# A fused adaLN block with its gradients: 128-row chunks for the modulation products, and masks, sums and output pieces moved in the tail

## The chip, the cores and the metric

The kernel runs on one core of one Trainium2 chip, in one launch. The metric is the time of an execution on the device in microseconds; lower is better. The core has a matrix engine (TensorE, PE in the profile, whose weight loads are listed as PEld), a vector engine (DVE), a scalar engine (ACT), GpSimd (POOL) and a queue engine (SyncE, SP) that issues most of the transfers here.

## The reference, cut to what matters

The block works on x of 2048 rows and 576 columns in bfloat16. A conditioning row c gives six modulation rows. The first branch, A, is a spectral filter; the second, B, is a bilinear gated unit with 4608 hidden columns.

```python
mod = (silu(c) @ w_mod).reshape(1, 6, 1, 576)        # c: 1 x 576, w_mod: 576 x 3456
sa, ca, ga, sb, cb, gb = (mod[:, i] for i in range(6))
h = layernorm(x) * (1 + ca) + sa
x = x + ga * irfft2(rfft2(h) * (w_r + 1j * w_i))     # branch A, w_r and w_i: 2048 x 289
h = layernorm(x) * (1 + cb) + sb
x = x + gb * (((h @ w_gate) * (h @ w_up)) @ w_down)  # branch B, w_gate and w_up: 576 x 4608
```

The outputs are this x and, for a given grad_out of the same shape, the gradients of the input x, w_r, w_i, w_gate, w_up, w_down, c and w_mod.

## The kernel before, in words

All on-chip data lie in one hand-planned buffer, which the profile calls `arena`; the eight banks of the matrix engine's output are `bank`. The order of TensorE's instructions is the order of the Python code. The other engines' instructions are put into an order by a scheduler, and each engine then runs its own list strictly in that order. SP issues its transfers from such a list, with eight rotating semaphores, so an issue can also wait for the transfer that was issued eight before it.

**Front (0 to about 160 us).** SP loads grad_out in four parts (`load_go`), x in four (`load_xs`), w_mod in three (`load_wm`: `wm_a` holds the row gb, `wm_b` sa and ca, `wm_c` ga, sb and cb), blocks of w_down (`load_wdn`) and the tables of the transforms (`TB`, `TC`, `TI`, `TBI`). Matmuls with one column turn c into columns (L269, L275, L278); ACT and DVE make silu(c) of them (`sc_bf`). The row gb is needed as a column, and L303 makes it from `wm_a`: five blocks of 128 columns, each a sum over six blocks of 96 rows of w_mod. The other five rows come from `mod_rows` (L328 to L340): for each half row of 288 columns, L333 adds six matmuls over blocks of 96 rows, with silu(c) repeated over 128 columns (`sc_rep`) as weights, so that every partition gets the row. ACT copies one half, DVE the other. `turn_go` transposes grad_out and `evac_go` copies it scaled by gb, `turn_wd` (L262) transposes w_down. The stages of the forward transform (`stage_a`, `stage_b`, `stage_c`, `stage_ci`, `stage_bi`, `stage_ai`) are interleaved with pieces of the product of grad_out and w_down.

**Middle (242 to 1190 us).** A loop over 18 chunks of 256 hidden columns computes branch B and the gradients of its weights.

**Tail (1190 us to the end).** Pieces of independent matmuls fill gaps. They stand in a queue, an object of class `Fill`: `run(us)` adds that many microseconds of credit and takes pieces, each with a nominal cost, until the credit is used up; `left()` is the nominal cost that is left; `flush()` takes all. Two kinds of pieces matter here. Gradient pieces compute the rest of the weight gradients of w_gate and w_up (eight matmuls of 256 or 288 columns, 0.87 us each). y pieces (`y_piece`, L1077) compute the product with w_down that makes the output x: 128 pieces of nine matmuls of 288 columns, 1.1 us each.

1. *Row loop*, 18 steps for 16 blocks of 128 rows. It ends the gradient of h (`gh2_last`), goes back through the second layer norm (`row_front`, `row_back`), adds column sums and products for the modulation gradients (`row_sums`) and starts the backward transform (`row_a`, with `stage_a`). Between them stand two calls `if fill.left() > 9.0: fill.run(1.0)` (L1141, L1145).
2. *Masks and sums.* `diag_mask` and `col_mask` (L1187 to L1203) cut diagonals out of the sums with DVE. Then eight matmuls (L1207) spread them over the partitions, and ACT copies the rows out (L1208).
3. *Spectral loop*, s = 0 to 8 (L1266 to L1298). Each step has `stage_b(s)` (L442), a transposition of the filter `W` (`turn`, L516), then for u = s - 1 `stage_c(u)` (L468, L504), `multiply` (DVE up to L528), the filter's gradient `grad_W` of the step before (DVE, L1249 to L1253) and `stage_ci(u)` (L555). Pieces stand between these by `fill.run`. At s = 1 the rest of the gradient pieces is taken, the queue is changed to the y pieces, and `X_d`, the spectrum that the forward part had stored in DRAM, is loaded for `grad_W` (`load_X`). The results of the gradient pieces are stored to DRAM (L888).
4. *Last loop*, j = 0 to 16 (L1330 to L1366). `stage_bi(j)`, then for row block j - 1 `stage_ai` (L572 and after), its copy out of the bank by ACT (L1341), the normalised x (L1343, made in the ring `x_r` of three buffers, into which SP loads x), the backward layer norm (`ln_bwd_a`, `ln_bwd_b`, with ACT's L1010 among its steps), and `column_sums` (L1031), with y pieces between by `fill.run(2.5)`, twice.
5. *End* (L1369 to L1401). The sums become columns, the gradient of w_mod's gb block is made (`o8l`), the gradient of c is computed from the transposed w_mod (L1391, L1397) and stored. y pieces stand in between by `fill.run(4.0)`.

Of the kernel before, what the change touches and what calls it, by code (L numbers as in the profile page):

```python
# [22 lines left out]
D = 576  # L23
# [58 lines left out]
def build(ctx, tc, A_x, A_w_r, A_w_i, B_w_gate, B_w_up, B_w_down, c_in, w_mod, grad_out,  # L82
# [22 lines left out]
    bank = psp.tile([128, 8, 512], FP32, name="bank")  # L105
# [44 lines left out]
    gbcol, c_f, sig = small[:, 66:71], small[:, 82:88], small[:, 88:94]  # L150
    nt = small[:, 100:108]
    smallb = V(8640, [32])
    c_bf, sc_bf, gb_bf, c2_bf = smallb[:, 0:6], smallb[:, 6:12], smallb[:, 12:17], smallb[:, 17:31]
    go = V(GO, [16, D])
    h2p = V(H2P, [16, 640])
    h2T = V(H2T, [16, 5, 128])
# [38 lines left out]
    TC = V(ACC + 2912, [9, 4, 128])  # L195
    TI = V(ACC + 12128, [9, 4, 128])
    TBI = V(ACC + 21344, [5, 288])
    wm_a, wm_b, wm_c = V(ST, [6, D]), V(ST + 71168, [6, 2 * D]), V(ST + 6912, [6, 3 * D])
    wm_t = {SGB: wm_a, SSA: wm_b[:, :, 0:D], SCA: wm_b[:, :, D:], SGA: wm_c[:, :, 0:D], SSB: wm_c[:, :, D:2 * D], SCB: wm_c[:, :, 2 * D:]}
    sc_rep = V(ST + 27648, [6, 128])  # L200
# [7 lines left out]
    with tc.manual_schedule(engines={PE}):  # L208
# [2 lines left out]
        ac.dma_start(BD.rearrange("p a b -> p (a b)"), tabs["BD"][:, :])  # L211

        def load_wm(t, s0, s1):
            sp.dma_start(t[0:96], w_mod[:, s0 * D:s1 * D].rearrange("(m q) n -> q m n", q=96))

        def load_go(jg):
            sp.dma_start(go[:, 4 * jg:4 * jg + 4, :], go_v[:, 4 * jg:4 * jg + 4, :])
# [1 line left out]
        def load_xs(jg):  # L219
            sp.dma_start(xs[:, 4 * jg:4 * jg + 4, :], x_v[:, 4 * jg:4 * jg + 4, :])  # L220
# [8 lines left out]
        load_go(2)  # L229
        load_go(3)  # L230
        load_xs(0)
        load_wm(wm_b, 0, 2)
        load_wdn(1)
        load_xs(1)
        load_xs(2)
        load_wdn(2)
# [26 lines left out]
                ac.copy(t[:, m0:m1, :].rearrange("p m f -> p (m f)"), pt[:, 0:256 * (m1 - m0)])  # L263


        q96 = slice(0, 96)
        cp = bank[:, 5, 128:160]
        for m in range(6):
            mm(cp[0:96, m:m + 1], c_row[0:1, 96 * m:96 * m + 96], ones[0:1, 0:1], True, True)  # L269
        ve.tensor_copy(c_f[q96], cp[q96, 0:6])  # L270
        act(sig[q96], c_f[q96], ACT.Sigmoid)
        tt(sc_bf[q96], c_f[q96], sig[q96], MUL)
        for h in range(2):
            for m in range(9):
                mm(cp[64 * h:64 * h + 64, 8 + m:9 + m], c_row[0:1, 64 * m:64 * m + 64], ones[0:1, 0:1], True, True)  # L275
        for m in range(5):
            n = 128 if m < 4 else 64
            mm(cp[0:n, 17 + m:18 + m], c_row[0:1, 128 * m:128 * m + n], ones[0:1, 0:1], True, True)  # L278

        def turn_go(jg, m):  # L280

# [17 lines left out]
            turn_go(0, m)  # L299
        for dk in range(5):  # L300
            d0 = 448 if dk == 4 else 128 * dk
            for m in range(6):
                mm(bank[:, 5, dk:dk + 1], wm_a[0:96, m, d0:d0 + 128], sc_bf[0:96, m:m + 1], m == 0, m == 5)  # L303
        ve.tensor_copy(gb_bf[:], bank[:, 5, 0:5])
        ve.tensor_copy(gbcol[:], gb_bf[:])
        c2f = small[:, 82:96]
        ve.memset(c2f, 0.0)
        ve.tensor_copy(c2f[:, 0:13], cp[:, 8:21])
        ve.tensor_copy(c2f[0:64, 13:14], cp[0:64, 21:22])
        for m in range(5):  # L310
            turn_go(1, m)
            evac_go(0, m)
# [1 line left out]
        for jg in (2, 3):  # L314
            for m in range(5):
                turn_go(jg, m)
                if jg == 3:
                    evac_go(1, m)
        for m in range(6):
            ve.tensor_copy(sc_rep[q96, m, :], sc_bf[q96, m:m + 1].to_broadcast([96, 128]))  # L320

        sbank = [0]

# [4 lines left out]
        def mod_rows(s):  # L328
            bias = 1.0 if s in (SCA, SCB) else 0.0
            for h in range(2):  # L330
                b = single()
                for m in range(6):
                    mm(bank[:, b, 0:288], sc_rep[0:96, m, :], wm_t[s][0:96, m, 288 * h:288 * h + 288], m == 0, m == 5)  # L333
                dst = mod[:, s, 288 * h:288 * h + 288]
                if h == 0:
                    act(dst, bank[:, b, 0:288], ACT.Copy, bias=bias)
                elif bias:
                    ts(dst, bank[:, b, 0:288], bias, None, ADD)
                else:
                    ve.tensor_copy(dst, bank[:, b, 0:288])  # L340

        def silu_columns():

            s2 = small[:, 50:64]
            act(s2, c2f, ACT.Sigmoid)
            tt(c2_bf[:, :], c2f, s2, MUL)
# [781 lines left out]
        for j in range(18):  # L1128
            want = min(16, 2 + 5 * j // 4)
            while done < want:  # L1130
                gh2_last(done)
                done += 1
                if done < want:
                    fill.run(1.0)
            while loaded < min(done, j + 3):
                load_n(loaded)
                loaded += 1
            if j < 16:
                row_front(j)
                row_back(j)  # L1140
            if fill.left() > 9.0:  # L1141
                fill.run(1.0)
            if 2 <= j < 18:
                row_sums(j - 2)
            if fill.left() > 9.0:  # L1145
# [12 lines left out]
        load_wdr(28, 36)  # L1158
        sring = [4, 5]


        for k in range(2):
            load_hl(k)
# [37 lines left out]

        m_sga, m_scb, m_ssb, gbh = diag_mask(5, 64), diag_mask(2, 0), col_mask(192), mk_r.next()
        ve.tensor_copy(gbh[:], gbacc[:])  # L1203
        for rows, hi, lo in ((rows23, m_sga, m_ssb), (rows45, m_scb, gbh)):
            for h in range(2):
                for q0, src in ((0, hi), (64, lo)):
                    mm(bank[q0:q0 + 64, 6 + h, 0:288], ones[:, 0:64], src[:, 288 * h:288 * h + 288], True, True)  # L1207
            ac.copy(halves(rows), bank[:, 6:8, 0:288])  # L1208
# [29 lines left out]
        for u in range(2):  # L1238
            Ws[u] = W_r.next()
            load_W(sp, Ws[u], u)  # L1240

        def load_X(u):
            Xls[u] = Xl_r.next()
# [86 lines left out]
        for j in range(17):  # L1330
# [6 lines left out]
            if j:  # L1337
                jj = j - 1
                stage_ai(Hs[jj])
                gh = gh_r.next()  # L1340
                ac.copy(halves(gh), bank[:, 2:4, 0:288])  # L1341
                n = xl[jj]
                act(n[:], n[:], ACT.Identity, bias=nmr1[:, jj:jj + 1], scale=rstd1[:, jj:jj + 1])  # L1343
# [116 lines left out]
```

## Time and profile before

| | us |
|---|---|
| median of four runs (1536.87, 1532.36, 1526.55, 1533.34) | 1532.85 |
| the profiled execution's own time | 1527.39 |
| its span, first to last instruction | 1525.5 |
| TensorE busy | 1476.6 |
| VectorE busy | 782.9 |
| ScalarE busy | 557.2 |
| GpSimd busy | 262.4 |

The profiled execution is one execution, and lies 5.5 us under the median of the runs. Times inside the profile count from the start of its span. A line such as "PE bank L555 <- DVE arena L528: 5.5, 4, 4.3" says that TensorE's instructions of line 555, which write a bank, waited four times for line 528 on VectorE, 5.5 us in total and 4.3 at the longest. A line of the stretches gives its bounds and length, then for each engine the busy time with the number of its instructions (PE, PEld, DVE, ACT, POOL), the clock granted to TensorE (1.00 is full), the DMA engines' share and the GB/s that they moved. A line of an engine's timeline gives the start, the duration, the instruction, and in brackets the idle time before it with what ended that.

### The profile page before, as it was taken

To read this page: it belongs to the slowest core of one execution; us is meant where nothing else is said; L and a number is where in the kernel's file an instruction comes from. 1 tells how busy PE (TensorE), PEld (TensorE's weight loads), DVE (VectorE), ACT (ScalarE), POOL (GpSimd) and SP (SyncE) were. 2 spreads that over 40 slices of the span, in tenths; PEclk is the share of its full clock that TensorE was granted. 3 is DMA by queue.
4 is the path that set the end of the run, shared out by engine and by line. 5 is a ranking of instruction groups with operands and counts; after the bars stand their busy time and mean duration, and the time that the engine had idled before them with its cause. 6 is when DMAs were issued, how large, how long until landed. Compare 5 with 4: busy or idle time off the path is not lost.

```text
span 1525.5 us, 28468 instructions
## 1 busy us (share of the span) xinstructions
PE 1476.6 (97%) x11295; PEld 987.5 (65%) x11295; DVE 782.9 (51%) x1733; ACT 557.2 (37%) x1062; POOL 262.4 (17%) x384
## 2 busy tenths in 40 slices
PE   7999998999999999999999999999999998899997
PEld 5444443677667668668668667767767676677665
DVE  6533596543443443453353353354354884787555
ACT  5766675212221221220320321221221674334665
POOL 1222322203202202202211211311301101000000
PEclk9999999999999999999999999999999999999999
DMA  9746886878548547557657646755844689798752
GB/s 295 217 142 160 231 229 165 216 113 189 125 93 185 132 109 162 134 113 156 146 113 145 159 115 130 165 122 119 173 116 92 166 217 290 188 242 206 199 165 86
DMA packets 440967, 248.65 MB, mean 163 GB/s; under 512 B 318401, under 2 KB 418306, under 8 KB 440322
## 3 DMA queue, kind: packets, MB, share of 16 engines
q1 hardware_dynamic: 417570, 176.43, 51.4%
q0 software_dynamic: 22496, 69.62, 15.0%
q8 instruction: 88, 1.44, 0.4%
q10 hardware_dynamic: 768, 0.79, 0.2%
q14 instruction: 45, 0.37, 0.1%
HBM read 96.46 MB, written 74.20 MB: 112 GB/s over the span
## 4 chain that ended last, share of the span: by engine, by line
PE 75%; issue 17%; DVE 3%; ACT 2%; DMA 2%; SPq 0%; POOL 0%; POOLq 0%; DVEq 0%; ACTq 0%
PE bank L802 9%; PE bank L833 8%; PE bank L804 8%; PE bank L880 8%; PE bank L884 8%; PE bank L939 5%; PE bank L942 5%; PE bank L941 5%; PE bank L940 5%; PE bank L370 3%; PE bank L374 3%; PE bank L797 3%; PE bank L900 2%; PE bank L858 1%; DMA arena<-in_B_w_down_dram 1%
## 5 line engine op out<-in xcount | busy, mean ns | idle before, releaser
L953 DVE TENSOR_TENSOR arena<-arena,bank 128x576 f32<-128x576 f32 x256 | 193.0, 754 | 305.2 <-PE bank L942 305.2
L808 ACT CAST arena<-bank 128x512 bf16<-128x512 f32 x144 | 84.3, 585 | 386.9 <-PE bank L798 375.3
L939 PE MATMUL bank<-arena 128*128 128x288 bf16 x576 | 164.6, 286 | 0.9 <-ACT arena L885 0.7
L942 PE MATMUL bank<-arena 128*128 128x288 bf16 x576 | 165.2, 287 | 0.0
L941 PE MATMUL bank<-arena 128*128 128x288 bf16 x576 | 165.0, 286 | 0.0
L940 PE MATMUL bank<-arena 128*128 128x288 bf16 x576 | 164.7, 286 | 0.0
L880 PE MATMUL bank<-arena 128*128 128x256 bf16 x1152 | 150.4, 274 | 0.5 <-ACT arena L885 0.5
L884 PE MATMUL bank<-arena 128*128 128x256 bf16 x1152 | 150.0, 273 | 0.0
L1077 PE MATMUL bank<-arena 128*128 128x288 bf16 x1152 | 149.7, 287 | 0.0
L802 PE MATMUL bank<-arena 128*128 128x512 bf16 x576 | 148.6, 380 | 0.0
L804 PE MATMUL bank<-arena 128*128 128x512 bf16 x576 | 147.8, 379 | 0.0
L1077 PEld LDWEIGHTS <-arena 128*128 128x128 bf16 x1152 | 111.8, 98 | 31.7 <-issue 3.3
L833 PE MATMUL bank<-arena 128*128 128x288 bf16 x1024 | 128.1, 286 | 0.0
L880 PEld LDWEIGHTS <-arena 128*128 128x128 bf16 x1152 | 111.2, 98 | 17.7 <-issue 4.4
L884 PEld LDWEIGHTS <-arena 128*128 128x128 bf16 x1152 | 112.6, 98 | 14.8 <-issue 1.3
L885 ACT CAST arena<-bank 128x256 bf16<-128x256 f32 x144 | 53.5, 372 | 185.8 <-PE bank L884 185.8
L833 PEld LDWEIGHTS <-arena 128*128 128x128 bf16 x1024 | 100.2, 98 | 28.2
L812 DVE TENSOR_TENSOR arena<-arena 128x512 bf16<-128x512 bf16 x144 | 61.2, 425 | 104.6 <-ACT arena L808 102.3
L802 PEld LDWEIGHTS <-arena 128*128 128x128 bf16 x576 | 50.3, 98 | 78.0 <-issue 30.4
L804 PEld LDWEIGHTS <-arena 128*128 128x128 bf16 x576 | 56.4, 98 | 67.9
L809 ACT CAST arena<-bank 128x512 bf16<-128x512 f32 x144 | 84.8, 589 | 23.1 <-PE bank L804 23.1
L382 ACT CAST arena<-bank 128x1024 bf16<-128x1024 f32 x72 | 72.7, 1013 | 42.0 <-PE bank L378 19.6
(254 smaller groups left out, 2249.0 us busy)
## 6 DMA issues: line engine op xcount, KB each, us to landing
ghh_d<-arena POOLq DMA_DIRECT2D x72, 256.0 KB, 3.8
arena<-ghh_d POOLq DMA_DIRECT2D x36, 512.0 KB, 5.6
hh_d<-arena SPq DMA_DIRECT2D x36, 512.0 KB, 4.5
arena<-hh_d SPq DMA_DIRECT2D x16, 1152.0 KB, 6.9
out_dram<-arena POOLq DMA_DIRECT2D x36, 256.0 KB, 5.1
arena<-in_B_w_down_dram POOLq DMA_DIRECT2D x18, 288.0 KB, 4.1
out_dram<-arena POOLq DMA_DIRECT2D x36, 144.0 KB, 5.5
arena<-in_B_w_gate_dram POOLq DMA_DIRECT2D x18, 256.0 KB, 3.5
```

The costliest lines, as they stand in the source:

```text
L802: mm(bank[:, bg, :], w[:, m, fs], h2T[:, js, m, :], odd == 0 and m == 0, odd == 1 and m == 3)
L804: mm(bank[:, bu, :], w[:, 4 + k, fs], h2T[:, js, m, :], odd == 0 and k == 0, odd == 1 and k == 3)
L809: ac.copy(u[:], bank[:, bu, :])
L833: mm(bank[:, b0 + h, 0:288], sf[:, 0, fb, j, :], go[:, j, 288 * h:288 * h + 288], j == 0, j == 15)
L880: mm(bank[:, st["b"], 0:256], h2p[:, j, 128 * m:128 * m + 128], sf[:, 1 + w, :, j, :], j == 0, False)
L884: mm(bank[:, st["b"], 0:256], h2p[:, j, 128 * m:128 * m + 128], sf[:, 1 + w, :, j, :], False, j == 15)
L939: mm(o, xT[:, 1, 0, cs], wT[p][:, 0, 0, hs], True, False)
L940: mm(o, xT[:, 2, 0, cs], wT[p][:, 0, 1, hs], False, False)
L941: mm(o, xT[:, 1, 1, cs], wT[p][:, 1, 0, hs], False, False)
L942: mm(o, xT[:, 2, 1, cs], wT[p][:, 1, 1, hs], False, True)
L953: tt(dst, dst, src, ADD)
L1077: mm(bank[:, yb, 0:288], hl[:, fb % 18, 128 * (j % 2):128 * (j % 2) + 128], wdr[:, fb, 288 * h:288 * h + 288], fb == 0, fb == 35)
```

## The change

The products with w_mod go over five blocks of rows, four of 128 and one of 64, in place of six of 96 (list `KC`). Each `load_wm` becomes two transfers. L303 has 25 matmuls for 30, L333 60 for 72, the column matmuls 23 for 29. The second block of w_down is loaded ahead of `wm_b`.

In the tail, the thresholds of the row loop go from 9.0 to 11.0, which in the built kernel keeps two gradient pieces longer: twelve for ten are left behind the row loop. The sums of L1207 and L1208 become a function `spread`, called twice in step s = 0 of the spectral loop with a gradient piece between; two gradient pieces stand ahead of `stage_b(0)`. At s = 1 the gradient pieces are all taken first, and three y pieces follow ahead of `stage_ci(0)`. The loads of w_down's last rows and of the first hidden rows (`load_wdr(28, 36)`, `load_hl`) are written after those of the filter.

In the last loop `fill.run(2.5)` becomes `fill.run(2.2)`, twice. In the built kernel each row block then has four y pieces; before, seven had four and nine had five. Two more y pieces are taken ahead of this loop, and eight for one stand in the end: four ahead of the R2 columns and four between them and L1391.

```diff
@@ load_wm
-            sp.dma_start(t[0:96], w_mod[:, s0 * D:s1 * D].rearrange("(m q) n -> q m n", q=96))
+            sp.dma_start(t[:, 0:4], w_mod[0:512, s0 * D:s1 * D].rearrange("(m q) n -> q m n", q=128))
+            sp.dma_start(t[0:64, 4], w_mod[512:576, s0 * D:s1 * D])
@@ loads
         load_xs(0)
+        load_wdn(1)
         load_wm(wm_b, 0, 2)
-        load_wdn(1)
@@ silu(c) as columns
-        q96 = slice(0, 96)
+        KC = [(0, 128), (128, 128), (256, 128), (384, 128), (512, 64)]
...
-        for m in range(6):
-            mm(cp[0:96, m:m + 1], c_row[0:1, 96 * m:96 * m + 96], ones[0:1, 0:1], True, True)
-        ve.tensor_copy(c_f[q96], cp[q96, 0:6])
-        act(sig[q96], c_f[q96], ACT.Sigmoid)
-        tt(sc_bf[q96], c_f[q96], sig[q96], MUL)
+        for m, (k0, n) in enumerate(KC):
+            mm(cp[0:n, 9 + m:10 + m], c_row[0:1, k0:k0 + n], ones[0:1, 0:1], True, True)
+        ve.tensor_copy(c2f[:, 9:13], cp[:, 9:13])
+        ve.tensor_copy(c2f[0:64, 13:14], cp[0:64, 13:14])
+        act(s2[:, 9:14], c2f[:, 9:14], ACT.Sigmoid)
+        tt(sc_bf, c2f[:, 9:14], s2[:, 9:14], MUL)
@@ gb as a column, mod_rows
-            for m in range(6):
-                mm(bank[:, 5, dk:dk + 1], wm_a[0:96, m, d0:d0 + 128], sc_bf[0:96, m:m + 1], m == 0, m == 5)
+            for m, (_, n) in enumerate(KC):
+                mm(bank[:, 5, dk:dk + 1], wm_a[0:n, m, d0:d0 + 128], sc_bf[0:n, m:m + 1], m == 0, m == 4)
...
-                for m in range(6):
-                    mm(bank[:, b, 0:288], sc_rep[0:96, m, :], wm_t[s][0:96, m, 288 * h:288 * h + 288], m == 0, m == 5)
+                for m, (_, n) in enumerate(KC):
+                    mm(bank[:, b, 0:288], sc_rep[0:n, m, :], wm_t[s][0:n, m, 288 * h:288 * h + 288], m == 0, m == 4)
@@ row loop (both places)
-            if fill.left() > 9.0:
+            if fill.left() > 11.0:
                 fill.run(1.0)
@@ masks and sums
-        for rows, hi, lo in ((rows23, m_sga, m_ssb), (rows45, m_scb, gbh)):
+        def spread(rows, hi, lo):
             for h in range(2):
@@ ahead of the spectral loop
             load_W(sp, Ws[u], u)
+        load_wdr(28, 36)
+        for k in range(2):
+            load_hl(k)
@@ spectral loop
             if s < 8:
+                if s == 0:
+                    fill.run(1.8)
                 Zs[s] = stage_b(s, ac_r, z_r)
                 fill.run(1.0)
                 if s:
                     turn(Ws[s], 6)
+                else:
+                    spread(rows23, m_sga, m_ssb)
                 fill.run(1.2)
+                if s == 0:
+                    spread(rows45, m_scb, gbh)
...
-                fill.run(5.0)
-                if s == 1:
+                if s > 1:
+                    fill.run(5.0)
+                else:
                     fill.flush()
                     fill = yfill
...
+                    fill.run(3.0)
                 stage_ci(u, Y_t, SD_t, Gt)
@@ last loop
-                fill.run(2.5)
-            fill.run(2.5)
+                fill.run(2.2)
+            fill.run(2.2)
```

More of the change, by code (lines that the diff above doesn't have):

```diff
@@ L149, in build @@
     rstd2, nmr2 = small[:, 50:66], small[:, 66:82]
-    gbcol, c_f, sig = small[:, 66:71], small[:, 82:88], small[:, 88:94]
+    gbcol = small[:, 66:71]
     nt = small[:, 100:108]
     smallb = V(8640, [32])
-    c_bf, sc_bf, gb_bf, c2_bf = smallb[:, 0:6], smallb[:, 6:12], smallb[:, 12:17], smallb[:, 17:31]
+    sc_bf, gb_bf, c2_bf = smallb[:, 0:5], smallb[:, 12:17], smallb[:, 17:31]
     go = V(GO, [16, D])
@@ L197, in build @@
     TBI = V(ACC + 21344, [5, 288])
-    wm_a, wm_b, wm_c = V(ST, [6, D]), V(ST + 71168, [6, 2 * D]), V(ST + 6912, [6, 3 * D])
+    wm_a, wm_b, wm_c = V(ST, [5, D]), V(ST + 71168, [5, 2 * D]), V(ST + 6912, [5, 3 * D])
     wm_t = {SGB: wm_a, SSA: wm_b[:, :, 0:D], SCA: wm_b[:, :, D:], SGA: wm_c[:, :, 0:D], SSB: wm_c[:, :, D:2 * D], SCB: wm_c[:, :, 2 * D:]}
-    sc_rep = V(ST + 27648, [6, 128])
+    sc_rep = V(ST + 27648, [5, 128])
     c_row = V(H2T + 6912, [D])
@@ L263, in turn_wd @@
                 ac.copy(t[:, m0:m1, :].rearrange("p m f -> p (m f)"), pt[:, 0:256 * (m1 - m0)])
-        q96 = slice(0, 96)
+        KC = [(0, 128), (128, 128), (256, 128), (384, 128), (512, 64)]
+        c2f, s2 = small[:, 82:96], small[:, 50:64]
+        ve.memset(c2f, 0.0)
         cp = bank[:, 5, 128:160]
-        for m in range(6):
-            mm(cp[0:96, m:m + 1], c_row[0:1, 96 * m:96 * m + 96], ones[0:1, 0:1], True, True)
-        ve.tensor_copy(c_f[q96], cp[q96, 0:6])
-        act(sig[q96], c_f[q96], ACT.Sigmoid)
-        tt(sc_bf[q96], c_f[q96], sig[q96], MUL)
+        for m, (k0, n) in enumerate(KC):
[4 more added lines that the diff above has]
+        tt(sc_bf, c2f[:, 9:14], s2[:, 9:14], MUL)
         for h in range(2):
             for m in range(9):
[L275 to L278, printed above, removed]
+                mm(cp[64 * h:64 * h + 64, m:m + 1], c_row[0:1, 64 * m:64 * m + 64], ones[0:1, 0:1], True, True)
         def turn_go(jg, m):
@@ L301, in build @@
             d0 = 448 if dk == 4 else 128 * dk
-            for m in range(6):
-                mm(bank[:, 5, dk:dk + 1], wm_a[0:96, m, d0:d0 + 128], sc_bf[0:96, m:m + 1], m == 0, m == 5)
+            for m, (_, n) in enumerate(KC):
+                mm(bank[:, 5, dk:dk + 1], wm_a[0:n, m, d0:d0 + 128], sc_bf[0:n, m:m + 1], m == 0, m == 4)
         ve.tensor_copy(gb_bf[:], bank[:, 5, 0:5])
         ve.tensor_copy(gbcol[:], gb_bf[:])
[L306 to L309, printed above, removed]
+        ve.tensor_copy(c2f[:, 0:9], cp[:, 0:9])
         for m in range(5):
@@ L318, in build @@
                     evac_go(1, m)
-        for m in range(6):
-            ve.tensor_copy(sc_rep[q96, m, :], sc_bf[q96, m:m + 1].to_broadcast([96, 128]))
+        for m in range(5):
+            ve.tensor_copy(sc_rep[:, m, :], sc_bf[:, m:m + 1].to_broadcast([128, 128]))
         sbank = [0]
@@ L331, in mod_rows @@
                 b = single()
-                for m in range(6):
-                    mm(bank[:, b, 0:288], sc_rep[0:96, m, :], wm_t[s][0:96, m, 288 * h:288 * h + 288], m == 0, m == 5)
+                for m, (_, n) in enumerate(KC):
+                    mm(bank[:, b, 0:288], sc_rep[0:n, m, :], wm_t[s][0:n, m, 288 * h:288 * h + 288], m == 0, m == 4)
                 dst = mod[:, s, 288 * h:288 * h + 288]
@@ L342, in silu_columns @@
         def silu_columns():
-            s2 = small[:, 50:64]
-            act(s2, c2f, ACT.Sigmoid)
-            tt(c2_bf[:, :], c2f, s2, MUL)
+            act(s2[:, 0:9], c2f[:, 0:9], ACT.Sigmoid)
+            tt(c2_bf[:, 0:9], c2f[:, 0:9], s2[:, 0:9], MUL)
             ve.tensor_copy(sc64, c2_bf[:, 0:9])
@@ L1144, in build @@
                 row_sums(j - 2)
-            if fill.left() > 9.0:
+            if fill.left() > 11.0:
                 fill.run(1.0)
@@ L1157, in build @@
                 sp.dma_start(TBI.rearrange("p a b -> p (a b)"), tabs["TBI"][:, :])
-        load_wdr(28, 36)
         sring = [4, 5]
-        for k in range(2):
-            load_hl(k)
         RA, RB = ST, ST + 84480
```

## The prediction

> **What bounds the kernel now.** I read the page's busy table first, then PE's waits, then the clock and the DMA rates in stretches. Page, part 1:
>
> ```profile
> PE 1476.6 (97%) x11295; PEld 987.5 (65%) x11295; DVE 782.9 (51%) x1733; ACT 557.2 (37%) x1062; POOL 262.4 (17%) x384
> ```
>
> TensorE is the bound: of 1525.5 us it is idle 49. The change can win only in idle time, in matmuls that vanish, and in slow clock. Waits of PE (who waited, for whom; total, times, longest):
>
> ```profile
> PE bank L555 <- DVE arena L528: 5.5, 4, 4.3
> PE bank L1031 <- DVE arena L1004: 3.8, 5, 0.8
> ...
> PE bank L262 <- DMA arena<-in_B_w_down_dram: 2.5, 1, 2.5
> ...
> PE bank L572 <- DVE arena L1366: 2.4, 1, 2.4
> PE bank L1031 <- ACT arena L1341: 2.2, 5, 0.8
> ...
> PE bank L516 <- DMA arena<-in_A_w_i_dram: 1.2, 1, 1.2
> PE bank L303 <- DMA arena<-in_w_mod_dram: 1.1, 1, 1.1
> ...
> PE bank L1207 <- ACT arena L1208: 0.7, 1, 0.7
> ...
> PE bank L1207 <- DVE arena L1199: 0.6, 1, 0.6
> PE bank L442 <- DVE arena L435: 0.6, 1, 0.6
> PE bank L516 <- DMA arena<-in_A_w_r_dram: 0.6, 1, 0.6
> ```
>
> Every part of the change aims at some of these: L303 and L262 at the front, L442, L1207 and L516 between the row loop and the spectral loop, L1031 in the last loop. Stretches (PE busy first; granted clock, DMA share and GB/s at the end):
>
> ```profile
> 9.00:13.00 4.00, 3.76 (x55) 3.68 (x52) 2.53 (x12) 2.69 (x4) 0.00 (x0) 1.00 1.04 420
> 16.00:19.00 3.00, 3.00 (x17) 1.09 (x16) 3.00 (x11) 2.75 (x3) 0.00 (x0) 1.00 1.04 223
> 32.00:34.00 2.00, 2.00 (x12) 0.67 (x11) 2.00 (x7) 0.96 (x2) 0.69 (x1) 1.00 1.03 225
> 39.00:42.00 3.00, 3.00 (x24) 1.62 (x22) 2.90 (x20) 3.00 (x6) 0.00 (x0) 1.00 1.01 419
> 23.34:26.74 3.40, 3.40 (x11) 0.82 (x10) 3.23 (x12) 3.04 (x5) 0.00 (x0) 0.50 1.05 410
> 237.30:241.80 4.50, 2.32 (x13) 0.99 (x11) 3.40 (x11) 4.50 (x6) 1.13 (x2) 1.00 0.94 252
> 1279.45:1282.85 3.40, 3.04 (x16) 1.34 (x15) 0.00 (x0) 0.95 (x2) 0.00 (x0) 0.50 1.19 296
> 1289.68:1293.09 3.41, 3.41 (x18) 2.37 (x16) 0.00 (x0) 1.01 (x2) 0.00 (x0) 0.50 1.14 329
> ```
>
> Two readings. The w_mod loads (96 partitions; alone in 16:19 and 32:34) move 223 to 225 GB/s, loads to 128 partitions 420. And shortly after small PE gaps the clock is halved for 3.41 us, which costs 1.7 us of work each.
>
> **Front (up to 160 us).** w_mod is 0.66, 1.33 and 1.99 MB in three loads. At 223 GB/s they take 2.9, 6.0 and 8.9 us, at 420 1.6, 3.2 and 4.7: 8.4 us less transfer. The tables and x beside it already use 128 partitions. Removed on PE: most of L303's wait (1.0); L262's 2.5, since w_down's second block landed at 22.06 behind the 6 us of wm_b and now goes ahead of it; the half-clock stretch at 23.34 just behind that gap (1.7); 12 of 72 matmuls at L333 (0.13 each, 1.6) and some twelve column matmuls (0.3). Sum 7.1. Added: three DMA issues on SP of about 0.5 us each (its rows take 0.4 to 1.0), in a queue that runs ahead of PE there. Not all of it arrives: from 36.5 to 55.75 ACT is busy without a pause, copying transposes and modulation rows, and DVE from 23.5 to 48.3, so a PE that comes early waits for their banks. I leave 2 to 2.5 for that: -4.5. The slow and the fast stretches differ in piece length too (grad_out, TC: 4.6 KB and more in one piece; w_mod 1.2 to 3.5 KB). If that is the cause, the loads get no faster, wm_c lands at 38.9 as before while PE comes some 4 us early and waits: about -2. So the front lies between -2 and -7.
>
> The rule that speaks against this: the Trainium skill, "DMA: Bandwidth & Descriptors", in "Why a DMA increments its semaphore by 16 and not by 1", says a tile of 96 partitions is spread over 16 engines just as one of 128 is. The stretches agree as far as they go: the DMA share is 1.04 in the slow and in the fast one. By the rule alone the front would give the -2 of the other reading. I take the rate of the rows.
>
> **Between rows and spectral loop (1272 to 1320).** Removed: the waits at L442 (0.63, masks), L1207 (0.73; the first one's 0.63 counts with the masks), L516 (0.62 and 1.15) as the sums no longer stand before stage_b(0) with nothing between them and their masks: 3.1. With those gaps go the two half-clock stretches at 1279.45 and 1289.68: 3.4. The work itself (16 sum matmuls, pieces of 0.87) is the same. Added: two gradient pieces less in front of row 15, so its last sums see DVE's chain with 1.75 less cover. That wait is not in the trace; its bounds are 0 and 2.6 (three pieces' time), I take 1.75, with a 0.7 chance of one half-clock stretch (1.2).
>
> Then the long wait. L555 of ci(1) waited 4.30 for DVE L528, which waited for X_d's load: the last gradient piece ends at 1298.2, its store lands at 1305.49, the load at 1308.48. So X_d comes 10.3 after the last piece, and DVE's L1249 starts at 1308.7. In the changed order of DVE's instructions grad_W(0) (L1249, L1250) stands ahead of z of s=2 (L488, L489), so the wait moves to stage_c(1). What PE has between the last piece and there is ci(0), four y pieces, stage_b(2), turn: 9.6 us; DVE's part after X_d makes the other side 13.8. So 4.2 against 4.3: no gain, and the two half-clock stretches at 1313.57 to 1320.40 (3.4) stay with it. Sum: -3.1 - 3.4 + 1.75 + 1.2 + 0 = -3.5, rounded to -3; range -6 (no new wait) to +1 (the row's wait at its bound, another stretch, X_d a microsecond later).
>
> The rule here: the Trainium skill, "TensorE: Matmul & The Clock Gate", "Why this matters for your kernels", wants no idle gaps over about 3 us. The trace differs: the clock fell after gaps of 1.64 and 1.74 (1244.74, 1202.83) and stayed at 1.00 after 2.18 (237.30:241.80 above). By the page only the 4.3 us gap would cost clock, and this part would come to -1. I use the rows.
>
> **Last loop and end.** Waits of L1031 sum to 6.0 in five rows. ACT shows why:
>
> ```profile
> 1478.77 0.87 ACT L1343 ACTIVATE arena<-arena 128x576 bf16<-128x576 bf16 x1 [1.88 <-DMA arena<-in_A_x_dram]
> 1479.54 0.85 ACT L1010 ACTIVATE arena<-arena 128x576 bf16<-128x576 bf16 x1
> 1480.30 0.38 ACT L1080 CAST arena<-bank 128x288 bf16<-128x288 f32 x1
> 1482.59 0.87 ACT L1343 ACTIVATE arena<-arena 128x576 bf16<-128x576 bf16 x1 [1.92 <-DMA arena<-in_A_x_dram]
> 1483.37 0.38 ACT L578 COPY arena<-bank 128x288 f32<-128x288 f32 x1
> 1483.64 0.64 ACT L1341 CAST arena<-bank 128x576 bf16<-128x576 f32 x1
> ```
>
> L1343 (a later row's x) stands ahead of L1341 (this row's evacuation) and waits for a load whose buffer L1010 has just freed. It is so in just the rows where L1031 waits. In the order of the changed build L1343 follows L1341 in all rows but one: the 6.0 go, about 1 remains. The y pieces themselves (1.1 each) only move: nine fewer in the rows, seven more at the end, two before. With less cover the DVE chain behind L572 (2.38) may be waited for up to 1.1 longer; I take 0.5. Sum -4.5, range -7 to +5. The far end is the rival below. End: four pieces before L1391 hide its 0.53, and the clock holds there: -0.8.
>
> **Sum.** -4.5 - 3 - 4.5 - 0.8 = -12.8, say -12.5: the profiled execution's 1527.39 (span 1525.5 and 1.9 around it) becomes 1515. It lies 5.5 below the median 1532.85, which is what is compared: 1532.85 - 12.5 = 1520.
>
> **Rivals.**
> B, half given back: w_mod no faster in 128 rows (front -2), a half-clock stretch behind a new gap (middle -1), loop -3, end -0.8: -6.8, 1526. For it: the clock fell after gaps of 1.6, so each new small wait can cost 1.7 more. Against it: every wait named above has a releaser that the change moves away. Chance 0.22.
>
> C, slower: the last loop is not paced by PE but by the x load ring and ACT. A row with four pieces lasts 5.95 without a wait and up to 7.86 with one; 14 rows took 102.4 before, and the pieces taken out go to the end or earlier and cost their 8.8 there (eight at 1.1). If the rows cannot run faster than the ring (free, load, normalise), they last 7.86, 110.0 in all: 7.6 + 8.8 = 16.4 instead of -4.5. With the other parts as forecast (-8.3) the time is 1532.85 + 8.1 = 1541. It decides from a row time of (102.4 - 8.8 + 8.3) / 14 = 7.28 on, where the whole is back at zero. Against it: a row of 7.05 with five pieces and no wait has ACT busy for 4.9 and DVE for 3.9, and rows of 5.95 exist. Chance 0.11.
>
> D, the front's gain is lost: ACT, busy from 36.5 to 55.75, ends there whatever PE does; front 0, others as forecast: -8.3, 1524.5. Against it: what ACT copies there is PE's output, which comes earlier too. Chance 0.12.
>
> **Numbers.** Forecast, 1520: 0.55; its own range, the half-widths of the parts (2.5, 3.5, 3) added in squares, is 5.2 either way. B and D lie at 1524 to 1526, C at 1541. Range: 1509 (the forecast's low end, and the 5 by which the runs before differ) to 1533 (takes in B and D with the same); C and the tails, 0.2, are left out. A change of 0.5% (7.7 us) is about what a measurement of this kernel can tell, so the limits are 1525.2 and 1540.5. Faster: 0.50 of the forecast, half of D, 0.08 of B: 0.64. Slower: 0.09 of C and 0.02 of tails: 0.11. Same: 0.25.
>
> **What would show it.** Right: L303 and L262 below 0.5; w_mod stretches near 400 GB/s and wm_c landed before 34; L333 60 times; no half-clock stretch between 1279 and 1293 of before; L1207 no wait; a wait of about 4 at stage_c(1) (L468 or L504) instead of L555; rows of the last loop at 6 to 6.2 and L1031 below 1.5 in total. Wrong: w_mod still at 225 and a new wait at the modulation rows; rows of 7 or more with x loads as releasers; new half-clock stretches behind row 15.

## The result and the profile after

The changed kernel takes 1527.41 us in the median of 43 runs (1524.18 to 1531.76), the kernel before 1530.68 in the median of 69. The ratio is 0.9979, with a 95% interval from 0.9973 to 0.9985: faster by about 3.2 us, where 12.5 were forecast; by the prediction's own limit (7.7 us) that counts as the same. The profiled execution of the changed kernel has a span of 1525.0 (1526.8 with what lies around it), so in the two profiles the difference is 0.5 only: the profile of before, 1527.39, is one of its shorter executions.

Part 1 of the changed kernel's page, busy time of the engines, shows nothing of it; TensorE is as full as before:

```profile
PE 1477.8 (97%) x11272; PEld 985.9 (65%) x11272; DVE 782.6 (51%) x1732; ACT 557.4 (37%) x1062; POOL 262.4 (17%) x384
```

PE's waits in the changed kernel (line numbers are 3 lower than before up to about line 1150, so L513 is the old L516, `turn`; L501 the old L504, `stage_c`; L1028 the old L1031; L569 the old L572; L1020 is a matmul of `row_sums`):

```profile
PE bank L513 <- DMA arena<-in_A_w_r_dram: 7.2, 2, 4.5
PE bank L501 <- DVE arena L486: 3.3, 1, 3.3
PE bank L1028 <- DVE arena L1001: 3.2, 3, 1.4
PE bank L569 <- DVE arena L1372: 3.1, 1, 3.1
...
PE bank L1020 <- DVE arena L1010: 1.9, 1, 1.9
```

Four of these five were in the forecast: row 15's new wait (1.9; 1.75 forecast), the wait for X_d moved to stage_c(1) (3.3; 4.2), what remains of the column sums (3.2; 1, so three times as much) and the wait at L569 (3.1; 2.9). Waits for L303's w_mod, for w_down's block (L262) and at the spreading sums are gone from the list. The first line is new, and the longest: TensorE waits 2.7 and 4.5 us for the spectral filter.

The trace divided at six places gives the ledger. The middle loop is taken from the first to the last matmul of its line L797 (L794 in the changed kernel), the row loop ends with the last matmul of `stage_a`, the last gradient piece with the last matmul of `gw_block`.

| stretch, us | before | changed | difference |
|---|---|---|---|
| start to first matmul of the middle loop | 243.42 | 239.32 | -4.10 |
| middle loop | 944.68 | 944.74 | +0.06 |
| row loop | 89.15 | 89.96 | +0.81 |
| to the last gradient piece | 21.13 | 18.19 | -2.94 |
| spectral loop, to the first stage_bi of the last loop | 98.19 | 108.17 | +9.98 |
| last loop, to the last column sum | 118.18 | 108.05 | -10.13 |
| end | 10.77 | 16.60 | +5.83 |

Each stretch up to the spectral loop came out near the forecast. The spectral loop gives it back: two y pieces more (2.2), 4.3 more idle time (12.24 for 7.92) and 6.8 us more at half clock (13.65 for 6.83), which costs half of that, 3.4. The sum is 9.9. Stretches of the changed kernel, in columns as before; in the first two nearly all packets are w_mod's (2304 and 3456 bytes), so they answer to the w_mod stretches of before, and the last three are half-clock stretches:

```profile
14.00:16.00 2.00, 2.00 (x19) 1.09 (x15) 1.99 (x4) 2.00 (x3) 0.00 (x0) 1.00 1.04 394
26.00:28.00 2.00, 2.00 (x11) 0.91 (x10) 2.00 (x6) 1.01 (x2) 0.00 (x0) 1.00 1.04 417
...
1306.12:1309.53 3.41, 3.41 (x16) 2.14 (x15) 3.41 (x7) 0.65 (x1) 0.00 (x0) 0.50 0.68 188
1333.43:1336.84 3.41, 3.41 (x16) 2.13 (x15) 0.00 (x0) 1.09 (x2) 0.00 (x0) 0.50 0.60 181
1364.15:1370.97 6.82, 4.95 (x21) 3.08 (x21) 0.00 (x0) 2.31 (x4) 0.00 (x0) 0.50 0.59 163
```

w_mod moves at 394 to 417 GB/s in 128 rows, as forecast. The last two half-clock stretches lie just at the two waits for the filter (PE starts again at 1332.88 and 1366.02); DVE is idle through both.

SP's own timeline shows where the filter load was. Kernel before (start, duration, issued transfer; `hh_d` are hidden rows, 1152 KB a load, `in_A_w` the filter, 144.5 KB a load):

```profile
1326.19 1.31 SPq L1223 DMA_DIRECT2D out_dram<-arena  x2
1328.25 0.59 SPq L511 DMA_DIRECT2D arena<-in_A_w_r_dram  x1
1328.93 0.58 SPq L511 DMA_DIRECT2D arena<-in_A_w_i_dram  x1
1329.61 4.28 SPq L1058 DMA_DIRECT2D arena<-hh_d  x2
```

The changed kernel:

```profile
1320.49 2.94 SPq L1055 DMA_DIRECT2D arena<-hh_d  x2
1325.52 3.03 SPq L1081 DMA_DIRECT2D out_dram<-arena  x1
1328.60 0.58 SPq L508 DMA_DIRECT2D arena<-in_A_w_r_dram  x1
1329.22 0.60 SPq L508 DMA_DIRECT2D arena<-in_A_w_i_dram  x1
```

When `multiply` frees the buffer is told by DVE, first the kernel before, then the changed one:

```profile
1327.43 0.76 DVE L521 TENSOR_TENSOR arena<-arena 128x1160 bf16<-128x1160 bf16 x1
...
1322.48 0.75 DVE L518 TENSOR_TENSOR arena<-arena 128x1160 bf16<-128x1160 bf16 x1
```

Before, unit 4's filter was issued at 1328.25, as soon as `multiply` had freed its buffer (L521 ended at 1328.19), and the pair of hidden-row loads followed. In the changed kernel the buffer was free at 1323.23 (end of L518), but the pair and the store of an output row stand ahead: the filter was issued at 1328.60 and landed at 1332.84. It is the three y pieces ahead of stage_ci(0) that do it, as the second experiment shows. A row pair of y pieces ends three pieces earlier against the spectral steps, and its end is what issues the next pair of hidden-row loads.

### The profile page after: what moved, and what is told of

Read it like the earlier page. It is cut to its first block, busy times and chain, and to the rows that moved or that the text cites. A ratio compares the mean times of both kernels' runs of the same rounds, so it can differ in the third digit from the quotient of the medians.

```text
span 1525.0 us, 28424 instructions
## 1 busy us (share of the span) xinstructions
PE 1477.8 (97%) x11272; PEld 985.9 (65%) x11272; DVE 782.6 (51%) x1732; ACT 557.4 (37%) x1062; POOL 262.4 (17%) x384
## 4 chain that ended last, share of the span: by engine, by line
PE 75%; issue 17%; DVE 3%; ACT 3%; DMA 2%; POOL 0%; SPq 0%; POOLq 0%; ACTq 0%; DVEq 0%
PE bank L799 9%; PE bank L830 8%; PE bank L801 8%; PE bank L877 8%; PE bank L881 8%; PE bank L936 5%; PE bank L939 4%; PE bank L938 4%; PE bank L937 4%; PE bank L367 3%; PE bank L371 3%; PE bank L794 3%; PE bank L897 2%; PE bank L374 1%; PE bank L855 1%
## 5 line engine op out<-in xcount | busy, mean ns | idle before, releaser
L830 PEld LDWEIGHTS <-arena 128*128 128x128 bf16 x1024 | 100.2, 98 | 28.2
L727 POOL DMA_DIRECT2D arena<-ghh_d x36 | 20.0, 554 | 393.9 <-DVE arena L808 387.1
```

Source lines behind the costliest of these rows:

```text
L830: mm(bank[:, b0 + h, 0:288], sf[:, 0, fb, j, :], go[:, j, 288 * h:288 * h + 288], j == 0, j == 15)
```

## The experiments

Theory S was: the order on SP makes the filter late. Rival T: the transfers themselves are slow. Differences in us are the ratio's distance from 1 times 1530.68.

**Filter loads on GpSimd** (changed kernel, one word):

```diff
-                    load_W(sp, Ws[u + 2], u + 2)
+                    load_W(po, Ws[u + 2], u + 2)
```

> The changed kernel with the filter loads of the backward spectral loop (units 2 to 7) issued by GpSimd in place of SP. Theory S (the order on SP): in the changed kernel two filter loads stand on SP behind a pair of hidden-row loads and an output store, and were issued 5 to 7 us after their buffer was free; on a queue of their own they are issued as soon as it is free. The wait of L513 for A_w_r, 7.2 in the changed kernel, falls below 1, half-clock stretches behind it go, the stretch from the last gradient piece to the last loop falls from 108.2 to 98 to 100, and the time is 6 to 9 us below the changed kernel, about 1519 to 1521. Rival T (the transfers are slow, since the DMA engines are crowded there): L513 still waits 5 or more, time as the changed kernel within 2 us.

Measured: 0.9941 (0.9923 to 0.9959), 9.0 below before and 5.8 below the changed kernel. The waits at L513 shrink to 0.3 and 0.2, the spectral loop to 100.2. As S said; but L501's wait grew to 5.2, so part of what PE gained it waited for at X_d, and the hidden-row loads were issued later here too (1323.39 and 1326.59), so this run alone doesn't separate the queue from the transfers.

**Without the three pieces** (changed kernel):

```diff
-                    fill.run(3.0)
                 stage_ci(u, Y_t, SD_t, Gt)
```

> The changed kernel without the three y pieces ahead of stage_ci(0) (they come three later in the queue). In SP's list the filter loads then stand ahead of the hidden-row loads again, as before. Theory S: L513's 7.2 falls below 1; but PE reaches stage_c(1) 3.3 us earlier, and X_d does not come earlier, so L501 (3.3) waits about 6.5; net 3 to 5 us below the changed kernel, with the clock stretches: 1522 to 1525. Rival T (crowded engines, whatever the order): L513 stays above 5, L501 at 6.5, and the time is about 3 above the changed kernel, 1531.

Measured: 0.9921 (0.9903 to 0.9940), 12.1 below before. No wait at L513 among the long ones; the spectral loop is 97.9. The wait for X_d fell at L552, 3.1, not 6.5: better than either theory. (L552 waits 8.2 in all; two more of its waits, 2.0 and 2.7, are explained under the middle below.) Removing three pieces of cover made the kernel 8.9 faster.

**Front alone, last loop alone** (each of them on the kernel before):

> The kernel before with the front of the change alone (five blocks of 128 rows, w_down's second block earlier). Theory: the profile's 4.1 us at the start of the middle loop is all of the front's gain and nothing behind it depends on it: first matmul of the middle loop at 239.3, the rest as before, time 4 below before: about 1527. Rival: the tail gives part of it back by its own waits or clock stretches: 1529 or more.

> The kernel before with fill.run(2.2) in the last loop alone (four y pieces in each row, the others at the end). The prediction's step: L1031's waits fall from 6.0 to 1 to 3, the wait at L572 grows to 3, L1391 has none; 2 to 5 us below before: 1526 to 1529. Rival C (rows paced by the x loads): rows of 7 or more, no gain or a loss: 1530 or more.

Measured: front 0.9948 (0.9931 to 0.9966), -8.0, twice the 4 that was expected; last loop 0.9965 (0.9953 to 0.9978), -5.4. Both alone beat the whole change, though the last loop's interval overlaps that of the whole. In the second the waits of the column sums fell from 6.0 to 2.0, and last loop and end together from 128.95 to 124.56. Rival C, rows paced by x loads, falls.

**The front in two** (on the kernel before; first the order alone, with 96 rows; then the 128 rows with the old order):

```diff
         load_xs(0)
+        load_wdn(1)
         load_wm(wm_b, 0, 2)
-        load_wdn(1)
```

> The kernel before with one edit: w_down's second block is loaded ahead of wm_b (w_mod still in 96 rows). The prediction's sum: L262's 2.5 and the half-clock stretch behind it (1.7) go, the w_mod transfers stay at 223 GB/s, so wm_c lands at 38.9 as before and PE, early, waits for it: front 1 to 2.5 us shorter. Rival: the order is all of the front's gain: the middle loop starts at 239.3, 4 us earlier, as in the changed kernel.

> The kernel before with w_mod in five blocks of 128 rows, w_down's second block still behind wm_b. The prediction's sum: w_mod moves at 400 GB/s, wm_b takes 3.3 in place of 6.0, so w_down's block lands near 19.3 and L262 waits 0 to 1; front 3 to 4 us shorter (middle loop at 239.5 to 240.5), nearly all of the front's gain. Rival (96 or 128 rows are equal, the order did it): w_mod stays below 250 GB/s, L262 still waits 2 or more, front 1 us shorter (fewer matmuls).

Measured: the order alone 1.0037 (1.0025 to 1.0050), 5.7 slower; the 128 rows alone 0.9952 (0.9937 to 0.9968), -7.3. The first shows the trap that the prediction named, deeper than it said. PE's waits of the run with the order alone:

```profile
PE bank L333 <- DMA arena<-in_w_mod_dram: 7.3, 2, 6.1
```

PE comes early and waits for w_mod, 1.3 for wm_b (landed at 24.24) and 6.1 for wm_c (42.71; 38.89 in the profile of before, 40.35 to 40.69 in the three other profiles with the same front), and the clock is halved for 10.2 us around the second wait. So the rows carry the front's gain, the faster transfer and the fewer matmuls together, which no run separates; with 96 rows the order only moves the wait from w_down to w_mod. In the second run w_down's block was waited for 1.0, as expected, but its middle loop starts at 243.0, not at 239.5 to 240.5: the profile shows 0.4 of the 7.3 that the times show, a first sign that the front of the profiled execution of before is a short one. In the changed kernel the two parts of wm_c landed at 32.37 and 33.47, and nobody waits for them.

**The middle in two** (on the kernel before: all of it but the three pieces; then the three pieces alone):

> The kernel before with the middle part of the change (thresholds 11.0, sums moved into step 0, loads of w_down's rest and hidden rows behind the filter's) but not the three y pieces ahead of stage_ci(0). The prediction's step: 3 us below before (waits at L442, L1207 and L516 go, one new wait of 1.9 at row 15). Rival: what it removes comes back as a longer wait for X_d at stage_c(1) or stage_ci(1): within 1 us of before.

> The kernel before with only the three y pieces ahead of stage_ci(0) added (and the gradient pieces taken out first there). SP's list then has a pair of hidden-row loads ahead of two filter loads, as in the changed kernel. Theory S: PE waits 5 to 7 us at L516, with half-clock stretches behind, and the wait for X_d (4.3) is 3 shorter; in sum 2 to 5 us above before. Rival: the phase of the pieces is harmless by itself and the waits at L516 need the earlier front or the moved sums: time 1 to 3 below before, L516 below 2.

Measured: 0.9993 (0.9980 to 1.0006) and 0.9997 (0.9982 to 1.0011): neither differs from before. In the first, row loop and sums took 2.3 less in the profile (107.99 for 110.28), as forecast, and then it was given back: the spectral loop took 0.7 more, since stage_ci waited 8.3 in four places for DVE (5.5 before), and the last loop 2.3 more (L1031 waits 7.5 in place of 6.0). The wait for X_d is not what grew, it fell from 4.3 to 2.7. What grew are the two waits of units 4 and 6 (0.2 each before):

```profile
1359.37 0.28 PE L555 MATMUL bank<-arena 128*128 128x256 bf16 x1 [2.37 <-DVE arena L528]
```

DVE's list has an item of the w_mod gradient (`mod_grad`, L1218) just ahead of `multiply` there (L520 at 1355.49), and that item waits for its load:

```profile
1352.64 0.76 DVE L1218 SCALAR_TENSOR_TENSOR arena<-arena 128x576 bf16<-128x576 bf16 x1 [1.66 <-DMA arena<-in_w_mod_dram]
```

Before, the item stood ahead of L488, one stage earlier (from 1347.58 on). At unit 6 it is the same, with 2.34 of waiting, and in the run without the three pieces, with 1.26 and 2.18. In the second, theory S's waits are there (L516, 1.3 and 3.7 for the filter) and the spectral loop is 9.2 longer, with two pieces more; but its last loop is 7.2 shorter with one piece less, since L1031 waits 1.2 in place of 6.0. The expected loss did not come: a shift of the pieces against the rows moved waits in both loops.

**Which of the two transfers ahead holds the filter** (changed kernel; hidden-row loads on GpSimd, then the output store on GpSimd):

```diff
-                                    load_hl(k)
+                                    load_hl(k, po)
```

> The changed kernel with the hidden-row loads that a y row triggers (L1055, k from 4 on) issued by GpSimd in place of SP; the filter loads and the output store stay on SP, the store still ahead of two filter loads. Theory S1 (the pair of hidden-row loads holds SP): L513's 7.2 falls below 2 and the time is 5 to 9 us below the changed kernel, about 0.994 of before. Rival S2 (the output store holds it, by its wait for DVE): L513 stays at 4 or more, time within 3 us of the changed kernel.

```diff
-                        sp.dma_start(o0_v[:, j, :], y[:])
+                        po.dma_start(o0_v[:, j, :], y[:])
```

> The changed kernel with the store of the output rows (L1081) issued by GpSimd; the hidden-row loads stay on SP ahead of two filter loads. Theory S1 (the hidden-row loads hold SP): L513 still waits 4 or more, time within 3 us of the changed kernel. Rival S2 (the store holds it): L513 below 2, 5 to 9 us below the changed kernel.

Measured: 1.0071 (1.0052 to 1.0089), 10.9 slower than before; and 0.9978 (0.9964 to 0.9992), as the changed kernel. The store is acquitted: with it gone, SP's timeline has

```profile
1320.03 3.15 SPq L1055 DMA_DIRECT2D arena<-hh_d  x2
1323.29 4.47 SPq L508 DMA_DIRECT2D arena<-in_A_w_r_dram  x1
1327.81 0.67 SPq L508 DMA_DIRECT2D arena<-in_A_w_i_dram  x1
```

and the wait stays (7.9): right behind the pair the issue itself took 4.47. The first run goes against theory S as it was put. SP was free and issued the filter early,

```profile
1322.77 0.59 SPq L508 DMA_DIRECT2D arena<-in_A_w_r_dram  x1
1323.46 0.56 SPq L508 DMA_DIRECT2D arena<-in_A_w_i_dram  x1
```

5.8 us earlier than in the changed kernel (1.6 of that by the run being ahead there: its pair was issued that much earlier); yet the second of them landed at 1335.07, 11.6 after its issue and 1.8 later than in the changed kernel, and PE's waits were

```profile
PE bank L513 <- DMA arena<-in_A_w_r_dram: 7.3, 2, 4.6
...
PE bank L513 <- DMA arena<-in_A_w_i_dram: 3.0, 2, 2.5
```

So it isn't SP that is taken but the DMA engines: the pair is 2.4 MB, and the engines are full with it and what goes beside it (share 1.02 to 1.08 at 280 to 296 GB/s from 1323 to 1335 in this run); at such a rate the pair alone takes 8 us. The run with the filter loads on GpSimd, with the pair on SP, shows the same from the other side:

```profile
arena<-in_A_w_r_dram POOLq DMA_DIRECT2D x1, 144.5 KB, 6.9
arena<-in_A_w_i_dram POOLq DMA_DIRECT2D x1, 144.5 KB, 6.7
```

Issued 0.5 and 1.3 after the second hidden-row load, the two parts landed 1.0 and 0.5 before it: beside the pair, from another queue, a small load is slow, but need not wait for all of it. The Trainium skill, "DMA: Bandwidth & Descriptors", says in "Issuing engines are not separate DMA queues" that transfers started by different engines run on the same 16 and interleave. The runs agree, with 11.6 and 6.9 for a load that takes 2.3 to 2.6 in the changed kernel where no hidden-row load is under way. Not all of the 14 us by which the first run lies above the changed kernel is the filter, though: its last loop is 8.7 longer, with waits of 4.6 at L569 and 3.9 at L1028 for ACT, and why is open.

**Front and last loop together; both mendings together:**

> The kernel before with the front and the last loop of the change, without its middle part. If the parts add up, the ratios of the two alone (0.9948 and 0.9965) give 0.991, about 13 us below before, and the middle part brings nothing on top. Rival (the parts share a gain, such as clock stretches or waits at L1031 that the earlier front moves already): 0.994 or more.

> The changed kernel without the three y pieces, and with the filter loads on GpSimd: the two mendings together, the candidate for the fastest. If what is left after either alone is the same wait (X_d, at stage_ci(1) or stage_c(1)), it is no faster than the version without the three pieces (0.992). If the filter loads still hold back something on SP there, it is 2 to 4 us faster: 0.990.

Measured: 0.9905 (0.9889 to 0.9920), -14.5: the two parts add up, and without the middle part the change does what the whole was forecast to do. The two mendings together give 0.9921 (0.9904 to 0.9937), no better than leaving out the three pieces alone.

**The filter written earlier** (changed kernel, three pieces kept; the load right behind `multiply`):

```diff
                 multiply(Xs[u], Ws[u], P1, P2, Y_t, SD_t, True, u)
+                if u + 2 < 8:
+                    Ws[u + 2] = W_r.next()
+                    load_W(sp, Ws[u + 2], u + 2)
...
                 stage_ci(u, Y_t, SD_t, Gt)
-                if u + 2 < 8:
-                    Ws[u + 2] = W_r.next()
-                    load_W(sp, Ws[u + 2], u + 2)
```

> The changed kernel, three pieces kept, with the filter load written right behind multiply in place of behind stage_ci. In SP's list unit 6's filter then stands ahead of the whole pair of hidden-row loads and unit 4's behind one of the two (in the changed kernel both stand behind both). Theory D (a filter load issued behind hidden-row loads lands only when these have landed, about 4 us for each of the two): the wait at turn for unit 6 (4.5) goes, that for unit 4 (2.7) falls below 1; the stretch from the last gradient piece to the last loop falls from 108.2 to 100 to 102; 0.993 to 0.995 of before. Rival (the three pieces cost by themselves, through the wait for X_d and the clock): waits at turn go but others take their place, 0.997 or more.

Measured: 0.9894 (0.9873 to 0.9915), -16.2, the fastest by its median, below the range of theory D; its interval overlaps those of front and last loop alone and of the run without the three pieces. SP's timeline of this run:

```profile
1319.59 0.55 SPq L1055 DMA_DIRECT2D arena<-hh_d  x1
1322.37 0.58 SPq L508 DMA_DIRECT2D arena<-in_A_w_r_dram  x1
1323.00 0.60 SPq L508 DMA_DIRECT2D arena<-in_A_w_i_dram  x1
1324.62 0.34 SPq L1081 DMA_DIRECT2D out_dram<-arena  x1
1325.06 0.39 SPq L1055 DMA_DIRECT2D arena<-hh_d  x1
```

With one hidden-row load ahead the filter's first part landed at 1327.85, 0.5 after that load, and in time. PE has no wait at L513, and the spectral loop takes 96.25 for 108.17, idle 4.9 for 12.2, with the same pieces. The only large wait in it is the one for X_d:

```profile
PE bank L501 <- DVE arena L486: 3.8, 2, 3.5
```

So theory D holds in the waits, and the order of the filter loads is worth 13.0 us (0.9894 against 0.9979). That the three pieces are good cover once they don't push the filter behind the hidden rows is what the profile says (54 y pieces in 96.25, where the run without the three has 52 in 97.9); the times of the two runs don't separate them.

**Front, last loop and the moved sums alone:**

> Front and last loop of the change, and of its middle part only the sums moved into step 0 (thresholds 9.0, no three pieces, loads in the old order). If the removed waits of 2.8 us at L442, L1207 and L516 count, 2 to 4 us less than front and loop alone (0.9905): 0.988 to 0.989. Rival (X_d sets when stage_ci(1) can start, so that time saved ahead of it is waited for there): 0.990 to 0.991, with L552's longest wait grown by what was saved.

Measured: 0.9938 (0.9916 to 0.9961), 5.1 slower than without the sums, with intervals that overlap a little. Neither case: it is mostly theory D in another place. PE, early, waits at turn for units 1 and 2:

```profile
PE bank L513 <- DMA arena<-in_A_w_i_dram: 4.4, 1, 4.4
PE bank L513 <- DMA arena<-in_A_w_r_dram: 4.1, 2, 2.8
```

Unit 1's filter (2.8) stood behind the first pair of hidden-row loads, which the change puts behind the filter and this kernel does not. Unit 2's first part, issued at 1296.82 behind another hidden-row load, landed at 1303.58, 1.0 after that load (1.3); its second part stood on SP behind X_d's load, which waits for the gradient pieces' store, and was issued at 1304.36 (4.4). The whole middle part without the three pieces has no such waits; it has both the reordered loads, which the prediction gave no price, and the higher thresholds, and no run separates the two. Nor is it shown that the moved sums pay then: the middle part alone is as the kernel before (0.9993), and on top of front and last loop it brings nothing (0.9921 against 0.9905).

## Why the prediction was wrong, point by point

- **Front, -4.5: too small.** The profile gave -4.1, the runs of it alone -8.0. The mechanism was right (w_mod at the rate of the fast rows, PE not waiting); what was off is the base. The profiled execution of before had the shortest front of four builds with the same front instructions: 243.42, where the others took 245.58, 247.83 and 248.11 (mean of the four 246.2; ten with the changed front lie between 239.19 and 242.40, mean 240.1). In the others wm_c landed at 40.35 to 40.69, not at 38.89; the two longest waited 0.9 and 2.0 for it at L333, a wait that the change removes, and had a half-clock stretch there (from 41.24 and 41.31) that the profile of before doesn't have. So the step that failed here is "It lies 5.5 below the median 1532.85, which is what is compared": the missing time was not spread over the kernel. These are four single executions; 6.1 of the 8.0 can be accounted for in this way.
- **The rule on partitions that the prediction cites** (the Trainium skill, "DMA: Bandwidth & Descriptors"). That 96 partitions use 16 engines as 128 do is not contradicted: the DMA share is 1.03 to 1.04 in both. But the rate followed the rows, 223 to 225 and 394 to 417, so the sum from the rows was the better one. The pieces have the same lengths in both kernels (2304 bytes in wm_b, 3456 in wm_c), so these did not make the difference that the prediction left open.
- **Rows and sums, -3.5: right for the stretch, not for the time.** -2.1 (row loop and sums together), with the new wait as sized (1.9); the clock behind that wait was halved for 6.83, which costs 3.4, where 1.2 was put in. But the middle part without the three pieces is as the kernel before (0.9993): what it saved was waited for further on, for DVE at stage_ci and at L1031 in the last loop. The prediction took a wait that goes for time that goes.
- **X_d, "4.2 against 4.3: no gain".** 3.3 at stage_c(1), moved as forecast. Right.
- **The rest of the spectral loop, no term.** This is the step that failed: +7.8 beyond the two pieces in the profile, and 13.0 in the times, when the filter loads alone are put back ahead. The prediction counted the three y pieces as cover and said of the pieces that they "only move". It listed the pieces' matmuls, not the transfers that the end of a row pair issues (the pair of hidden-row loads), and did not follow what these pass on the way: two filter loads. The orders of SP's instructions in both builds show it; the prediction argued from DVE's and ACT's orders there, not from SP's.
- **Luck.** Without the three pieces the change measures -12.1, close to the forecast -12.5. That is two errors that cancel: the front gave 3.5 more than forecast, the middle 3 less.
- **Last loop and end, -5.3.** -5.4 alone: the reading of ACT's order (L1343 ahead of L1341) was right. In the changed kernel, ACT's timeline shows the evacuation (L1347) first and the x that waits for its load (L1349) after it; in this row L1028 waits 1.4 all the same, for DVE:

```profile
1432.35 0.40 ACT L575 COPY arena<-bank 128x288 f32<-128x288 f32 x1
1432.64 0.65 ACT L1347 CAST arena<-bank 128x576 bf16<-128x576 f32 x1
1434.39 0.87 ACT L1349 ACTIVATE arena<-arena 128x576 bf16<-128x576 bf16 x1 [1.10 <-DMA arena<-in_A_x_dram]
```

- **Rivals.** B had the size nearly right (half given back) for other reasons: w_mod did get faster, and its loop was not the one that gave back. C and D fell.
- **Two small slips** that change nothing: the spreading sums are 8 matmuls, not 16, and DVE pauses for 1.3 at 27.1 within the stretch "from 23.5 to 48.3".

What stays open: why the scheduler put the w_mod gradient's items later in DVE's list there, and how much of the last loop's gain hangs on the phase of the pieces (the three alone took its waits from 6.0 to 1.2).

## What to carry to other kernels

When filler work is moved, list its transfers beside its matmuls, and compare the order of the transfers that come with it against every small load with a deadline. On the same queue the small load landed 0.8 and 1.1 after the large ones ahead of it in the changed kernel; beside two large ones from another queue it took 6.4 to 12.4 in place of 2.3 to 2.6. The load with a deadline was best written at the place where its buffer comes free. And a wait that goes is time gained only if no later wait grows by it, as with the middle part here. Before a gain is subtracted, look whether the profiled execution has its usual share of the wait that goes; if it lies below the median, it may be the wait that is short there.

## What was not expected of the hardware

A 144.5 KB load takes 2.3 to 2.6 us in the changed kernel where no hidden-row load is under way, 10.2 to 12.4 on SP beside two 1152 KB loads from GpSimd, and 6.4 to 6.9 on GpSimd beside two from SP. With those two on SP and the output store away, the issue of the load behind them took SP 4.47 and 5.11 where 0.4 to 0.6 is usual. And the length of a gap doesn't tell whether the clock falls: in the changed kernel 2.19 at 235.44 and 2.66 at 252.73 left it at full, 1.86 at 1251.39 halved it for 3.41 and 1.92 at 1271.87 for 6.83. In the run with the filter written earlier the same gap at the same place (2.19, up to 236.62) has it halved from 236.43 for 3.41.
